# A gated scan with top-k experts on one core: who weighs the scan's input, how the expert weights lie in memory, and where the last scatter may write

## The chip, the cores and the metric

The kernel runs on one core of one Trainium2 chip. The metric is device time in microseconds, the median of several executions. One execution was also recorded by the profiler; all rows below come from it.

## The reference

For each of 4 batches, 6208 tokens of width 256 pass through a gated scan, and then the 128 tokens with the highest score pass through a small two-layer expert. Cut to what matters:

```python
# x, f_logit: [4, 6208, 256] f32; w1: [256, 1024]; w2: [1024, 256]; capacity 128
f = lower_bound + (1.0 - lower_bound) * sigmoid(f_logit)
for t in range(S):
    h = f[:, t] * h + (1.0 - f[:, t]) * x[:, t]
    y[:, t] = h
scores = einsum('bsd,d->bs', y, w_gate)
out = y.copy()
for b in range(B):
    top = argpartition(-scores[b], capacity)[:capacity]
    ye = maximum(y[b, top] @ w1, 0.0) @ w2
    out[b, top] = y[b, top] + sigmoid(scores[b, top])[:, None] * ye
```

## The kernel before

The host lays x and f_logit out with the 256 channels on partitions (two halves of 128) and tokens along the free dimension. A batch is cut into 7 units of 1 to 4 blocks of 256 tokens; the first unit of a batch also takes the 64 tokens left over. There are 28 units and so 56 halves, numbered s = 0 to 55 (unit i has the halves 2i and 2i+1). Halves are 576, 768, 832, 1024 or 256 tokens wide.

For each unit the SyncE queue (SP) loads the forget logits into a tile `ft` (`load_f`, L319; 4 buffers) and x into a tile `xt` (`load_x`, L326; 6 buffers), up to 1 MB each. Then, with r = sigmoid(-f_logit) and ol = 1 - lower_bound:

- `gate` (ScalarE, L335) writes r over `ft` for the whole unit;
- `forget` (ScalarE, L342) writes f = 1 - ol * r into `gt`, a tile in PSUM with two buffers, so it waits for the scan of the half two before;
- the scan's input (1 - f) * x = ol * r * x is made in `xt`. For most halves GpSimd (POOL) does it in two instructions, `prepare` (L345: x * ol) and `weigh` (L353: times r from `ft`). For the seven halves in `SWIFT`, VectorE (DVE) does it in one (L351: x * ol * r, both tensors in SBUF). For the last two halves (`direct`), r is written to PSUM, f back into `ft`, and VectorE reads r from PSUM (L333, L339, L349);
- `scan` (VectorE, L356) runs h = f * h + input along the tokens, f from PSUM, in place in `xt`.

TensorE multiplies the result with the gate vector (`scores`, L369) and transposes it (`turn`, L390). ScalarE copies it to `ym` (`put`, L413; 10 buffers), and SP stores `ym` to the output (`store`, L424; the left-over tokens L427). When a batch's scores are there, VectorE and TensorE search the threshold (`choose`), and `experts` runs: GpSimd gathers the 128 rows from the output in HBM (`fetch`, L736), TensorE transposes them (`flip`, L741) and multiplies with w1 (`up`, L776) and w2 (`down`, L787), VectorE mixes (`mix`, L791), GpSimd scatters the rows back (`scatter`, L795). `flip` of a batch waits for `mix` of the batch before. For the last batch, `fetch` comes behind one tiny memset for each of the last 6 stores (L804), each of which waits until its store has landed.

The weights w1 and w2 (1 MB each) are loaded once (L839, L840), in lines of 4 KB and 1 KB. The last batch finds its rows in a faster way that can be in doubt; then its scatter goes to 128 spare rows behind the end of the output, and a branch does all batches anew. The spare rows are first written by one DMA (`spare_rows`, L836) behind the last store.

The order of every engine's instructions is fixed when the program is built: a planner (`Plan.run`) lists all operations with an engine, an assumed cost, a rank and what they wait for, plays them through, and emits them in the order that comes out. On the chip each engine, and SP's queue too, takes its instructions strictly in that order. Ranks are 10 * s and an offset (`AHEAD` for loads, `STORE` for stores, `TURN` and `PUT` for transposes and their copies, `EXPERT` and `FIND` per batch). `BACKLOG` says how much work the planner lets SP queue ahead. The lines that matter most for SP's order:

```python
add("sp", 0.05 + 2.45 * k, load_f, p - AHEAD, [("weigh", ef), ("scan" if ef < DIRECT[0] else "forget", ef), ("f", i - 1)], ("f", i), late=DONE)
add("sp", 0.05 + 2.45 * k, load_x, p - AHEAD + 1, [("f", i), ("turn", ex - 1), ("turn", ex), ...], ("x", i), late=DONE)
add("sp", ..., store, 20.0 * i + STORE[b] - RUSH.get(i, 0.0), [("put", s), ("put", s - 1), ("store", i - 1)], ("store", i), late=DONE)
```

Here `ef` is the second half of the unit that had the same `ft` buffer, four units before.

Of the kernel before, what the change touches and what calls it, by code (L numbers as in the profile page):

```python
# [17 lines left out]
P = 128  # L18
# [9 lines left out]
DIRECT = (0, 2)  # L28
SWIFT = (9, 13, 17, 21, 25, 29, 53)
XBUF, FBUF, YBUF = 6, 4, 10  # L30
AHEAD = 40.0
BACKLOG, STORE = 3.0, [200.0, 200.0, 200.0, 200.0]
EASED = 1000
LATE, PIECE, SOON, NEAR = 2, 4, 100.0, 5
BIG = ()
TURN, PUT, KEEP, FIND, EXPERT = 0.0, 20.0, 10.0, [0.0, -20.0, -60.0, -100.0], [150.0, 90.0, 100.0, 0.0]
WEIGHTS_AT = 90.0
RUSH = {13: 20.0}
# [22 lines left out]
class Plan:  # L61
# [107 lines left out]
def gated_scan_moe(tc, x, fl, lb, wg, wr, w1, w2, outs, cap):  # L169
    nc = tc.nc  # L170
    v, a, pe, g = nc.vector, nc.scalar, nc.tensor, nc.gpsimd
    with ExitStack() as ctx:
# [128 lines left out]
        def half(s):  # L301
# [8 lines left out]
            direct = s < DIRECT[0] or s >= N - DIRECT[1]  # L310
# [19 lines left out]
            def gate():  # L330
                if direct:
                    gs[s] = pf.tile([P, 4 * BLK], F32, name="gt")
                    a.activation(gs[s][:, :n], fs[s], ACTF.Sigmoid, scale=-1.0)  # L333
                else:
                    a.activation(whole[i], whole[i], ACTF.Sigmoid, scale=-1.0)  # L335

            def forget():
                if direct:
                    a.activation(fs[s], gs[s][:, :n], ACTF.Identity, scale=nl[:, h : h + 1], bias=1.0)  # L339
                    return  # L340
                gs[s] = pf.tile([P, 4 * BLK], F32, name="gt")
                a.activation(gs[s][:, :n], fs[s], ACTF.Identity, scale=nl[:, h : h + 1], bias=1.0)  # L342
# [88 lines left out]
            if h == 0:  # L431
                ef, ex = NH * (i - FBUF) + 1, NH * (i - XBUF) + 1
                oddb = units[i - XBUF] if i >= XBUF else None
                add("sp", 0.05 + 2.45 * k, load_f, p - AHEAD, [("weigh", ef), ("scan" if ef < DIRECT[0] else "forget", ef), ("f", i - 1)], ("f", i), late=DONE)
                add("sp", 0.05 + 2.45 * k, load_x, p - AHEAD + 1, [("f", i), ("turn", ex - 1), ("turn", ex), ("scores", ex), ("odd", oddb[0]) if oddb and oddb[3] else None], ("x", i), late=DONE)
            if direct:
                add("act", 0.15 + 0.85 * k, gate, p, [("f", i), ("scan", s - 2), ("forget", s - 1)], ("gate", s))
                add("dve", 0.15 + 1.07 * k, weigh, p, [("gate", s), ("x", i)], ("weigh", s))
            else:
                if h == 0:  # L440
                    add("act", 0.1 + 0.88 * 2 * k, gate, p, [("f", i)], ("gate", s))
                else:
                    plan.alias(("gate", s), ("gate", s - 1))
                if form == "pool" and s not in SWIFT:
                    add("pool", 0.1 + 1.1 * k, prepare, p, [("x", i)], ("ready", s))
                add("dve" if s in SWIFT else "pool", 0.15 + (1.07 if s in SWIFT else 2.2) * k, weigh, p, [("gate", s), ("ready", s), ("x", i)], ("weigh", s))
            add("act", 0.15 + 0.93 * k, forget, p, [("gate", s), ("scan", s - 2)], ("forget", s))
# [264 lines left out]
        def experts(b, pick=None):  # L712
# [184 lines left out]
        add("sp", 5.0, weights, WEIGHTS_AT, [], ("w",), late=DONE)  # L897
# [26 lines left out]

# [22 lines left out]
```

## Time and profile before

| what | value |
|---|---|
| device time, median of 3 runs | 217.18 us (216.74 to 218.33) |
| the profiled execution's own time | 216.66 us |
| its span, first to last instruction | 214.9 us |
| busy share of the span | PE 78%, DVE 79%, ACT 75%, POOL 77% |
| moved by DMA | 79.84 MB, mean 372 GB/s over the span |
| granted TensorE clock | 0.998 |

The span is the stretch that the rows below count from 0; the profiled execution's own time is 1.8 us longer than the span. A busy share is a mean over the whole span, with a filled stretch and an emptier tail; the GB/s of a stretch say how well the DMA engines were used in it.

### The profile page before, as it was taken

The page shows a single profiled execution, that of the slowest core. Times are in us where ns is not written, and L with a number is a line of the kernel's source. Part 1 is how long each engine was busy: PE and PEld are TensorE (multiplying, and loading weights), DVE is VectorE, ACT ScalarE, POOL GpSimd, SP SyncE. Part 2 cuts the span into 40 slices and gives each one's busy share as a digit, 9 for nine tenths or more (in the row PEclk, how much of TensorE's full clock was granted, in tenths as well). Part 3 has the DMA queues.
Part 4 walks back from the last instruction along what each step waited for, and adds up shares of the span by engine and source line. Part 5 has one row for each costly group of instructions (what it writes and reads, how often), then busy time and mean ns, then how long its engine had stood idle before and what let it go on. Part 6 is the DMA issues. An engine that isn't in the chain of part 4 may idle for free.

```text
span 214.9 us, 3576 instructions
## 1 busy us (share of the span) xinstructions
PE 166.7 (78%) x1188; PEld 106.2 (49%) x1188; DVE 169.2 (79%) x359; ACT 160.3 (75%) x226; POOL 165.2 (77%) x166
## 2 busy tenths in 40 slices
PE   0299986857998879588979967669879878999690
PEld 0043643524455435344548836435547556758570
DVE  2656497979999999999899989688898999891100
ACT  3778899997899899599899778987989378621110
POOL 6699999999795989996999999999999951001201
PEclk9999999999999999999999999999999999999999
DMA  5999999999999999999999999999999999993100
GB/s 179 390 427 421 429 415 392 395 415 419 419 424 418 420 423 418 287 392 412 417 423 422 423 427 421 426 422 421 411 419 411 431 421 424 425 424 117 49 5 31
DMA packets 14568, 79.84 MB, mean 372 GB/s; under 512 B 1873, under 2 KB 3282, under 8 KB 8018
## 3 DMA queue, kind: packets, MB, share of 16 engines
q1 hardware_dynamic: 13872, 78.52, 89.5%
q0 software_dynamic: 384, 1.05, 1.3%
q8 instruction: 11, 0.18, 0.3%
q14 instruction: 11, 0.09, 0.1%
q10 hardware_dynamic: 290, 0.00, 0.1%
HBM read 53.48 MB, written 26.08 MB: 370 GB/s over the span
## 4 chain that ended last, share of the span: by engine, by line
DVE 26%; DMA 25%; POOL 20%; issue 11%; ACT 7%; PE 6%; POOLq 1%; SPq 0%; another core or an unknown queue 0%; DVEq 0%; ACTq 0%
DMA ft<-fl 15%; DVE xt L356 14%; POOL xt L353 12%; POOL xt L345 8%; DMA out<-ym 6%; ACT ft L335 3%; DVE xt L351 3%; DVE ft L627 3%; DMA xt<-x 3%; ACT gt L342 2%; PE pt L390 2%; PE pm L787 2%; ACT ym L413 1%; DMA out<-res,idx 1%; PE pm L776 1%
## 5 line engine op out<-in xcount | busy, mean ns | idle before, releaser
L356 DVE TENSOR_TENSOR_SCAN xt<-gt,xt 128x1024 f32<-128x1024 f32 (+3 forms) x54 | 112.5, 2096 | 17.0 <-POOL xt L353 15.4
L353 POOL TENSOR_TENSOR xt<-xt,ft 128x1024 f32<-128x1024 f32 (+3 forms) x47 | 100.3, 2139 | 4.8 <-POOL xt L345 1.2
L390 PE MATMUL pt<-ident,xt 128*128 128x128 f32 (+1 forms) x392 | 66.7, 305 | 4.6 <-ACT ym L413 3.7
L390 PEld LDWEIGHTS pt<-ident,xt 128*128 128x128 f32 (+1 forms) x392 | 52.7, 202 | 26.2 <-ACT ym L413 15.5
L342 ACT ACTIVATE gt<-ft,nl 128x1024 f32<-128x1024 f32 (+3 forms) x54 | 55.5, 1030 | 9.8 <-DVE xt L356 6.1
L413 ACT COPY ym<-pt 128x512 f32<-128x512 f32 (+1 forms) x104 | 53.7, 556 | 10.0 <-PE pt L390 9.2
L345 POOL TENSOR_SCALAR xt<-xt,ol 128x1024 f32<-128x1024 f32 (+3 forms) x47 | 51.9, 1107 | 8.2 <-DMA xt<-x 6.0
L369 PE MATMUL score<-xt,wgr 128*32 128x256 f32 x380 | 35.7, 403 | 23.9 <-DVE xt L356 20.4
L335 ACT ACTIVATE ft<-ft 128x2048 f32<-128x2048 f32 (+3 forms) x27 | 46.5, 1722 | 5.7 <-DMA ft<-fl 5.5
L906 PE MATMUL score<-wgr 128*32 128x256 f32 x114 | 31.2, 390 | 0.0
L369 PEld LDWEIGHTS score<-xt,wgr 128*32 128x32 f32 x380 | 9.0, 110 | 36.5 <-DVE xt L356 29.5
L776 PE MATMUL pm<-xT,w1t 128*128 128x128 f32 x128 | 16.2, 281 | 0.0
L776 PEld LDWEIGHTS pm<-xT,w1t 128*128 128x128 f32 x128 | 14.9, 192 | 1.7 <-ACT xT L745 0.8
L787 PE MATMUL pm<-w2t,hT 128*128 128x256 f32 x64 | 14.9, 383 | 0.0
L906 PEld LDWEIGHTS score<-wgr 128*32 128x32 f32 x114 | 10.1, 109 | 9.4 <-issue 1.6
L787 PEld LDWEIGHTS pm<-w2t,hT 128*128 128x128 f32 x64 | 11.7, 191 | 1.5
L351 DVE SCALAR_TENSOR_TENSOR xt<-xt,ol,ft 128x1024 f32<-128x1024 f32 (+2 forms) x7 | 12.1, 1723 | 0.0
L791 DVE SCALAR_TENSOR_TENSOR res<-pm,open,xe 128x256 f32<-128x256 f32 x4 | 1.9, 481 | 12.3 <-PE pm L787 12.3
L804 POOL MEMSET ym<- 1x1 f32 x6 | 0.6, 94 | 13.6 <-DMA out<-ym 11.1
L736 POOL DMA_INDIRECT xe<-out,idx x4 | 4.4, 1100 | 7.9 <-DMA out<-ym 6.6
L782 ACT ACTIVATE hT<-pm 128x512 f32<-128x512 f32 x8 | 4.8, 594 | 5.1 <-PE pm L776 5.1
L795 POOL DMA_INDIRECT out<-res,into x1 | 1.0, 979 | 9.4 <-DVE res L791 9.4
(153 smaller groups left out, 109.7 us busy)
## 6 DMA issues: line engine op xcount, KB each, us to landing
ft<-fl SPq DMA_DIRECT2D x17, 1024.0 KB, 11.2
xt<-x SPq DMA_DIRECT2D x17, 1024.0 KB, 12.8
out<-ym SPq DMA_DIRECT2D x17, 1024.0 KB, 13.3
out<-ym SPq DMA_DIRECT2D x7, 768.0 KB, 15.4
ft<-fl SPq DMA_DIRECT2D x6, 768.0 KB, 8.2
xt<-x SPq DMA_DIRECT2D x6, 768.0 KB, 9.6
ft<-fl SPq DMA_DIRECT2D x3, 576.0 KB, 10.5
xt<-x SPq DMA_DIRECT2D x3, 576.0 KB, 8.6
```

What stands on the lines that cost most here:

```text
L335: a.activation(whole[i], whole[i], ACTF.Sigmoid, scale=-1.0)
L342: a.activation(gs[s][:, :n], fs[s], ACTF.Identity, scale=nl[:, h : h + 1], bias=1.0)
L345: g.tensor_scalar(xs[s], xs[s], ol[:, h : h + 1], 1.0, ALU.mult, ALU.mult)
L351: v.scalar_tensor_tensor(xs[s], xs[s], 1.0 if form == "pe" else ol[:, h : h + 1], fs[s], ALU.mult, ALU.mult)
L353: g.tensor_tensor(xs[s], xs[s], fs[s], ALU.mult)
L356: v.tensor_tensor_scan(xs[s], fs[s] if direct else gs[s][:, :n], xs[s], carry[h] if blk0 else 0.0, ALU.mult, ALU.add)
L369: pe.matmul(score[j * CG : (j + 1) * CG, b % 2], row(b, h, r), xs[s][:, c : c + BLK], start=(h == 0 and r == 0), stop=(h == NH - 1 and blk ...
L390: pe.transpose(out, src, ident)
L413: copy(yms[i][:, j0:j1, rows], pts[s, j0][:, : (j1 - j0) * P].rearrange("p (j d) -> p j d", d=P))
L776: pe.matmul(st["pm", f // TP][:, c : c + P], w1t[:, h, f * P : (f + 1) * P], st["xT"][:, h], start=(h == 0), stop=(h == NH - 1))
L787: pe.matmul(st["py"][:, :D], st["hT"][:, f], w2t[:, f], start=(f == 0), stop=(f == NF - 1))
L906: pe.matmul(score[:CG, 0], wgr[:, 0, CG : 2 * CG], wgr.rearrange("p a c -> p (a c)"), start=False, stop=True, skip_group_check=True)
```

## The change

Fourteen halves in place of nine are weighed by VectorE, now from f in PSUM: it computes (f - 1) * x, which is minus the scan's input, and the scan subtracts it. So such a half doesn't read `ft` after `forget`, and its weigh waits for `forget`. The special form of the last two halves goes. The weights are folded by the host so that each partition reads one line of 8 KB. The last scatter is given the end of the output as a bound and skips indices beyond it, so the spare rows and the DMA that writes them go. Some of the planner's assumed costs and constants change, so the order on every queue is planned anew.

```diff
-DIRECT = (0, 2)
-SWIFT = (9, 13, 17, 21, 25, 29, 53)
+SWIFT = (0, 1, 2, 3, 9, 13, 17, 21, 25, 29, 33, 53, 54, 55)
-BACKLOG, STORE = 3.0, [200.0, 200.0, 200.0, 200.0]
+BACKLOG, STORE = 4.0, [200.0, 200.0, 200.0, 200.0]
-LATE, PIECE, SOON, NEAR = 2, 4, 100.0, 5
+LATE, PIECE, SOON, NEAR = 4, 2, 100.0, 5
-TURN, PUT, KEEP, FIND, EXPERT = 0.0, 20.0, 10.0, [0.0, -20.0, -60.0, -100.0], [150.0, 90.0, 100.0, 0.0]
+TURN, PUT, KEEP, FIND, EXPERT = 10.0, 30.0, 10.0, [0.0, -20.0, -60.0, -100.0], [60.0, 120.0, 200.0, 0.0]
...
             def weigh():
-                if direct:
-                    v.scalar_tensor_tensor(xs[s], xs[s], 1.0 if form == "pe" else ol[:, h : h + 1], gs[s][:, :n], ALU.mult, ALU.mult)
-                elif s in SWIFT:
-                    v.scalar_tensor_tensor(xs[s], xs[s], 1.0 if form == "pe" else ol[:, h : h + 1], fs[s], ALU.mult, ALU.mult)
+                if swift:
+                    v.scalar_tensor_tensor(xs[s], gs[s][:, :n], 1.0, xs[s], ALU.subtract, ALU.mult)
                 else:
                     g.tensor_tensor(xs[s], xs[s], fs[s], ALU.mult)
 
             def scan():
-                v.tensor_tensor_scan(xs[s], fs[s] if direct else gs[s][:, :n], xs[s], carry[h] if blk0 else 0.0, ALU.mult, ALU.add)
+                v.tensor_tensor_scan(xs[s], gs[s][:, :n], xs[s], carry[h] if blk0 else 0.0, ALU.mult, ALU.subtract if swift else ALU.add)
...
-                add("sp", 0.05 + 2.45 * k, load_f, p - AHEAD, [("weigh", ef), ("scan" if ef < DIRECT[0] else "forget", ef), ("f", i - 1)], ("f", i), late=DONE)
+                add("sp", 0.05 + 2.45 * k, load_f, p - AHEAD, [*(("weigh", q) for q in (ef - 1, ef) if q not in SWIFT), ("forget", ef), ("f", i - 1)], ("f", i), late=DONE)
...
+            if swift:
+                add("dve", 0.15 + 1.07 * k, weigh, p - HASTE, [("forget", s), ("x", i)], ("weigh", s))
+            else:
+                add("pool", 0.1 + 1.03 * k, prepare, p, [("x", i)], ("ready", s))
+                add("pool", 0.15 + 2.22 * k, weigh, p, [("gate", s), ("ready", s), ("x", i)], ("weigh", s))
+            add("act", 0.15 + 0.97 * k, forget, p, [("gate", s), ("scan", s - 2)], ("forget", s))
...
-                g.indirect_dma_start(out=outs[b][:, :], out_offset=to, in_=st["res"][:cap, :], in_offset=None)
+                g.indirect_dma_start(out=outs[b][:, :], out_offset=to, in_=st["res"][:cap, :], in_offset=None,
+                                     **(dict(bounds_check=S - 1, oob_is_err=False) if planned and b == B - 1 else {}))
...
-        def spare_rows():
-            nc.sync.dma_start(outs[B - 1][S:, :], wgr.rearrange("p a c -> p (a c)"))
-
         def weights():
-            nc.sync.dma_start(w1t, w1.rearrange("(h p) f -> p h f", p=P))
-            nc.sync.dma_start(w2t, w2.rearrange("(k p) d -> p k d", p=P))
+            nc.sync.dma_start(w1t.rearrange("p h f -> p (h f)"), w1)
+            nc.sync.dma_start(w2t.rearrange("p k d -> p (k d)"), w2)
...
-        add("sp", 0.3, spare_rows, 1e6, [("store", len(units) - 1)], ("spare",), late=DONE)
...
+def folded(w):
+
+    return np.ascontiguousarray(w.reshape(-1, P, w.shape[1]).transpose(1, 0, 2).reshape(P, -1))
```

The halves 0 to 3 and 33 move from GpSimd to VectorE; 9, 13, 17, 21, 25, 29 and 53 stay on VectorE in the new form; 54 and 55 were the two `direct` ones.

## Rows read from the trace of the kernel before

**Rows 1.** The page's second part: GB/s in 40 equal slices of 5.37 us.
```profile
GB/s 179 390 427 421 429 415 392 395 415 419 419 424 418 420 423 418 287 392 412 417 423 422 423 427 421 426 422 421 411 419 411 431 421 424 425 424 117 49 5 31
```

**Rows 2.** Busy time by stretch; the last three columns: clock, DMA share, GB/s.
```profile
36.00:40.00 4.00, 2.65 (x27) 1.64 (x28) 4.00 (x3) 4.00 (x7) 3.92 (x3) 1.00 1.08 367
40.00:84.00 44.00, 35.58 (x272) 20.67 (x271) 42.10 (x82) 40.31 (x56) 39.46 (x27) 1.00 1.02 420
84.00:92.00 8.00, 5.75 (x43) 3.08 (x42) 7.86 (x11) 5.70 (x8) 7.75 (x8) 1.00 0.93 307
92.00:192.00 100.00, 83.40 (x630) 55.75 (x629) 89.94 (x207) 79.40 (x117) 79.60 (x56) 1.00 1.01 421
```

**Rows 3.** Timeline of SP's queue, w2's load and around 80 us: start, us, instruction.
```profile
24.13 0.46 SPq L840 DMA_DIRECT2D w2t<-w  x1
...
75.58 0.33 SPq L319 DMA_DIRECT2D ft<-fl  x1
...
76.55 0.77 SPq L424 DMA_DIRECT2D out<-ym  x1
...
85.68 0.33 SPq L319 DMA_DIRECT2D ft<-fl  x1
```

**Rows 4.** SP's own waits from 60 to 96 us: total, times, longest.
```profile
SPq L319 <- DVE xt L351: 15.9, 3, 8.2
```

**Rows 5.** Timeline of GpSimd, ScalarE and VectorE beside two of VectorE's weighs.
```profile
28.64 2.33 DVE L351 SCALAR_TENSOR_TENSOR xt<-xt,ol,ft 128x1024 f32<-128x1024 f32 x1
...
29.87 2.09 POOL L345 TENSOR_SCALAR xt<-xt,ol 128x1024 f32<-128x1024 f32 x1
...
79.75 4.70 POOL L353 TENSOR_TENSOR xt<-xt,ft 128x1024 f32<-128x1024 f32 x2 [0.80 <-POOL xt L345]
...
82.56 1.12 ACT L342 ACTIVATE gt<-ft,nl 128x1024 f32<-128x1024 f32 x1
...
83.21 2.32 DVE L351 SCALAR_TENSOR_TENSOR xt<-xt,ol,ft 128x1024 f32<-128x1024 f32 x1
```

**Rows 6.** Groups by line and shape: count, busy us, mean ns, idle before.
```profile
L356 DVE TENSOR_TENSOR_SCAN xt<-gt,xt 128x1024 f32<-128x1024 f32 x34 | 79.1, 2342 | 8.0 <-POOL xt L353 7.9
...
L353 POOL TENSOR_TENSOR xt<-xt,ft 128x768 f32<-128x768 f32 x11 | 21.0, 1912 | 1.1 <-ACT ft L335 0.4
...
L345 POOL TENSOR_SCALAR xt<-xt,ol 128x768 f32<-128x768 f32 x11 | 9.9, 905 | 0.3 <-DMA xt<-x 0.3
L351 DVE SCALAR_TENSOR_TENSOR xt<-xt,ol,ft 128x1024 f32<-128x1024 f32 x5 | 9.7, 1938 | 0.0
...
L627 DVE SCALAR_TENSOR_TENSOR ft<-gt,most 128x768 f16<-128x768 f32 x7 | 6.7, 956 | 0.4 <-PE gt L624 0.2
...
L349 DVE SCALAR_TENSOR_TENSOR xt<-xt,ol,gt 128x256 f32<-128x256 f32 x2 | 0.9, 470 | 0.2 <-ACT ft L339 0.2
```

**Rows 7.** DMA issues by line, the load of w2: KB, us from issue to landing.
```profile
w2t<-w SPq DMA_DIRECT2D x1, 1024.0 KB, 17.1
```

**Rows 8.** Timeline of the tail; in brackets the idle time before and its releaser.
```profile
188.39 0.61 SPq L424 DMA_DIRECT2D out<-ym  x1
...
189.05 1.07 SPq L836 DMA_DIRECT2D out<-wgr  x1
...
192.76 0.16 DVE L640 SCALAR_TENSOR_TENSOR idx<-pulled 128x1 int32<-128x1 f32 x1
...
197.04 0.09 POOL L804 MEMSET ym<- 1x1 f32 x1 [0.57 <-DMA out<-ym]
...
198.12 0.97 POOL L736 DMA_INDIRECT xe<-out,idx  x1 [0.99 <-DMA out<-wgr]
...
198.87 0.48 DVE L791 SCALAR_TENSOR_TENSOR res<-pm,open,xe 128x256 f32<-128x256 f32 x1 [4.30 <-PE pm L787]
...
200.96 0.41 PE L741 MATMUL pm<-ident,xe 128*128 128x128 f32 x2 [1.65 <-DMA xe<-out,idx]
...
210.00 0.98 POOL L795 DMA_INDIRECT out<-res,into  x1 [9.36 <-DVE res L791]
```

More of the change, by code (lines that the diff above doesn't have):

```diff
@@ L27 @@
 FORMS = [["pool", "pool"]] * 4
-DIRECT = (0, 2)
-SWIFT = (9, 13, 17, 21, 25, 29, 53)
+SWIFT = (0, 1, 2, 3, 9, 13, 17, 21, 25, 29, 33, 53, 54, 55)
 XBUF, FBUF, YBUF = 6, 4, 10
 AHEAD = 40.0
-BACKLOG, STORE = 3.0, [200.0, 200.0, 200.0, 200.0]
+BACKLOG, STORE = 4.0, [200.0, 200.0, 200.0, 200.0]
 EASED = 1000
-LATE, PIECE, SOON, NEAR = 2, 4, 100.0, 5
+LATE, PIECE, SOON, NEAR = 4, 2, 100.0, 5
 BIG = ()
-TURN, PUT, KEEP, FIND, EXPERT = 0.0, 20.0, 10.0, [0.0, -20.0, -60.0, -100.0], [150.0, 90.0, 100.0, 0.0]
+TURN, PUT, KEEP, FIND, EXPERT = 10.0, 30.0, 10.0, [0.0, -20.0, -60.0, -100.0], [60.0, 120.0, 200.0, 0.0]
 WEIGHTS_AT = 90.0
+HASTE = 0.0
 RUSH = {13: 20.0}
@@ L309, in half @@
             k = n / 1024
-            direct = s < DIRECT[0] or s >= N - DIRECT[1]
+            swift = s in SWIFT
             form = FORMS[b][h]
@@ L330, in gate @@
             def gate():
-                if direct:
[L332 to L335, printed above, removed]
+                a.activation(whole[i], whole[i], ACTF.Sigmoid, scale=-1.0)
             def forget():
-                if direct:
-                    a.activation(fs[s], gs[s][:, :n], ACTF.Identity, scale=nl[:, h : h + 1], bias=1.0)
-                    return
                 gs[s] = pf.tile([P, 4 * BLK], F32, name="gt")
@@ L347, in weigh @@
             def weigh():
-                if direct:
-                    v.scalar_tensor_tensor(xs[s], xs[s], 1.0 if form == "pe" else ol[:, h : h + 1], gs[s][:, :n], ALU.mult, ALU.mult)
-                elif s in SWIFT:
-                    v.scalar_tensor_tensor(xs[s], xs[s], 1.0 if form == "pe" else ol[:, h : h + 1], fs[s], ALU.mult, ALU.mult)
+                if swift:
+                    v.scalar_tensor_tensor(xs[s], gs[s][:, :n], 1.0, xs[s], ALU.subtract, ALU.mult)
                 else:
@@ L433, in half @@
                 oddb = units[i - XBUF] if i >= XBUF else None
-                add("sp", 0.05 + 2.45 * k, load_f, p - AHEAD, [("weigh", ef), ("scan" if ef < DIRECT[0] else "forget", ef), ("f", i - 1)], ("f", i), late=DONE)
+                add("sp", 0.05 + 2.45 * k, load_f, p - AHEAD, [*(("weigh", q) for q in (ef - 1, ef) if q not in SWIFT), ("forget", ef), ("f", i - 1)], ("f", i), late=DONE)
                 add("sp", 0.05 + 2.45 * k, load_x, p - AHEAD + 1, [("f", i), ("turn", ex - 1), ("turn", ex), ("scores", ex), ("odd", oddb[0]) if oddb and oddb[3] else None], ("x", i), late=DONE)
-            if direct:
-                add("act", 0.15 + 0.85 * k, gate, p, [("f", i), ("scan", s - 2), ("forget", s - 1)], ("gate", s))
-                add("dve", 0.15 + 1.07 * k, weigh, p, [("gate", s), ("x", i)], ("weigh", s))
-            else:
[L440 to L447, printed above, removed]
+                add("act", 0.1 + 0.9 * 2 * k, gate, p, [("f", i)], ("gate", s))
+            else:
+                plan.alias(("gate", s), ("gate", s - 1))
+            if swift:
[4 more added lines that the diff above has]
+            add("act", 0.15 + 0.97 * k, forget, p, [("gate", s), ("scan", s - 2)], ("forget", s))
             add("dve", 0.1 + 2.24 * k, scan, p, [("forget", s), ("weigh", s), ("scan", s - 2)], ("scan", s))
@@ L896, in gated_scan_moe @@
             half(s)
-        add("sp", 5.0, weights, WEIGHTS_AT, [], ("w",), late=DONE)
+        add("sp", 4.9, weights, WEIGHTS_AT, [], ("w",), late=DONE)
         add("pe", 0.4, spread_row, -1e3, [("x", 0)], ("row",), frees=("kept row",))
         add("act", 0.37, keep_row, -1e3, [("row",)], ("kept row",))
-        add("sp", 0.3, spare_rows, 1e6, [("store", len(units) - 1)], ("spare",), late=DONE)
         for b in range(B):
@@ L936 @@
         "wr": np.ascontiguousarray(moe_w_gate.reshape(1, D)),
-        "w1": np.ascontiguousarray(moe_w1),
-        "w2": np.ascontiguousarray(moe_w2),
+        "w1": folded(moe_w1),
+        "w2": folded(moe_w2),
     }
@@ L941 @@
     args = [nc.dram_tensor(n, arr.shape, F32, kind="ExternalInput").ap() for n, arr in arrays.items()]
-    outs = [nc.dram_tensor(f"out{b}", (S + P * (b == B - 1), D), F32, kind="ExternalOutput").ap() for b in range(B)]
+    outs = [nc.dram_tensor(f"out{b}", (S, D), F32, kind="ExternalOutput").ap() for b in range(B)]
     with tile.TileContext(nc, schedule_with_timeline_sim=True) as tc:
```

## Prediction

> **What bounds the kernel now.** I read the page's slices first, because a busy share over the whole span hides stages. The transfer rate is near 420 GB/s from the second slice to 193 us, except for one slice of 287 and its neighbour of 392, with shallower dips to 395 and 392 around 32 to 43 us [rows 1]. The table by stretch sharpens that: 420 over 40 to 84 us, 421 over 92 to 192 us, at a DMA share of 1.0, but 307 over 84 to 92 us and 367 over 36 to 40 us [rows 2]. No compute engine is that full. So the DMA stream sets the time to about 197 us, and what counts is bytes, slow bytes and holes in it.
>
> SP's queue shows where the hole comes from. After a load at 75.58 us and a store at 76.55 us it issues nothing until 85.68 us [rows 3]; its own waits name VectorE's weigh L351, with 8.2 us as the longest [rows 4]. That weigh reads `ft`, so the next load into the buffer waits for it, and the stores behind the load in SP's fixed order wait too. When SP goes on, the engines have run low.
>
> The tail comes third. The last store is issued at 188.39 us and the spare rows at 189.05 us; the last of the tiny memsets, which waits for the last store, runs at 197.04 us, and the last gather only at 198.12 us, after 0.99 us of waiting for the spare rows' DMA [rows 8]. Gather, expert and scatter then run in series to the end, hidden by nothing.
>
> **The change, part by part.**
>
> *Spare rows gone.* The gather needs the last store but no longer the DMA that overlapped it in name only: 0.99 us off the tail [rows 8]. What is late next is the expert of batch 2: its mix ends at 198.87 + 0.48 = 199.35 us, and the last expert's transposes, which wait for it, ran at 200.96 us [rows 8]. So up to 1.6 us may be gained in front of this mix without touching it; what goes beyond needs the mix to move as well. It should: its gather waits for a store, which moves with the stream.
>
> *Weights in 8 KB lines.* w2, in 1 KB lines, was issued at 24.13 us [rows 3] and landed 17.1 us later, at 41.2 us [rows 7], so it moved at the end of that stretch. At 36 to 40 us the rate was 367 with a DMA share of 1.08: the engines were full but slow. Against the 421 of the long stretch that is (421 - 367) / 421 x 4 = 0.5 us [rows 2]. I take 0.5, with 0 and, for the edges of the dip, 0.8 as ends. The Trainium skill speaks against it: "DMA: Bandwidth & Descriptors", section Specifications, puts line rate at transfers of 512 B and more, so 1 KB lines would cost nothing, folding would gain nothing, and the sum below would be 0.5 us smaller. The row says otherwise.
>
> *The hole.* Its price is (421 - 307) / 421 x 8 = 2.2 us [rows 2]. The load that ended it waited for the weigh that ran 83.21 to 85.53 us. In the new form it would wait for `forget`, done at 82.56 + 1.12 = 83.68 us, and for GpSimd's weigh of the half before, done at 79.75 + 4.70 = 84.45 us [rows 5]. That alone is 1.1 us earlier with nothing else moved. The engines ahead of it move too. VectorE was busy 42.1 of 44 us over 40 to 84 us [rows 2], so what it saves there lets buffers go earlier. A weigh of 1024 took 1.94 us on average [rows 6] and up to 2.33, and one beside it on GpSimd, L345, took 2.09 us [rows 5], against some 905 x 1024 / 768 = 1.2 us by its narrower form [rows 6]: they held each other up.
>
> *The new weigh.* No row shows this form at 1024. The two nearest, with one operand in PSUM, are L349 (256 wide, 0.47 us) and L627 (768 wide, 0.956 us) [rows 6]; their slope, 0.95 ns per element, gives 1.20 us at 1024 and 0.77 at 576 (estimates). Both ran while GpSimd did next to nothing, so the other end is the contended 2.33 us [rows 5]. I take 1.20: the scan, too, has one operand in PSUM and one in SBUF, and holds a mean of 2.34 us over 34 instances beside GpSimd [rows 6]. [...]
>
> For the seven halves that stay (five of 1024, one 768, one 576) that is 5 x 1.20 + 0.96 + 0.77 = 7.7 us in place of some 12.1 (the five of 1024 took 9.7 [rows 6]). The five that come to VectorE (0 to 3, 33: two of 576, three of 768) cost 2 x 0.77 + 3 x 0.96 = 4.4 us. So VectorE's total stays as it is, with relief in the first search and new work at the start, where GpSimd held it up. GpSimd loses three halves at 0.905 + 1.912 = 2.8 us [rows 6] and two of 576 at three quarters of that, 12.7 us in all, and the mutual hold-ups. Beside the DMA stream all this is worth nothing by itself; it counts only through the hole.
>
> *New wait.* A weigh on VectorE now waits for `forget`, which waits for the scan two halves before. Queued behind it on VectorE are the next scans and search steps, and TensorE and SP's buffers wait for those. `forget` took 1.12 us [rows 5] and the scan between takes 2.34 [rows 6], so it is ready in time unless ScalarE is late. I cost it at nothing; without that cover it is up to 1.1 us for each of the 14, and matters only where VectorE is already full.
>
> *The scan that subtracts, the gate of the last unit, the bound on the scatter.* The same pass with another operation: 0. The last unit's gate and weigh sit some 10 us ahead of the last store's landing, behind queued stores: 0. The scatter at 210.00 us takes 0.98 us to issue [rows 8]; the bound may cost between nothing and as much again, 1.0, and a little below nothing can't be excluded. I take 0, since nothing suggests a second pass over the indices.
>
> *The new order.* It is not in the trace. The planner's assumed costs and constants change for every queue, so the hole may vanish, shrink or reappear elsewhere. Of 2.2 us I take 1.7, nearer to the full price than to the 1.1 us of the dependence alone.
>
> **Sum.** 1.0 (spare rows) + 0.5 (weights) + 1.7 (hole) = 3.2 us off 216.66 us for an execution like the profiled one. That one lies 0.5 us under the median of the runs, so the median goes from 217.18 to 214.0 us.
>
> **Rivals.**
>
> *The hole stays.* SP blocks again for longer than what it has queued. For it: SP's order is fixed, and stores stand behind loads. Against it: the awaited weigh is shorter and no longer what `ft` waits for. Only 1.5 us remain: 215.7.
>
> *The gain is given back by batch 2's expert.* `EXPERT` ranks it behind the last transposes now (200 in place of 100). If its mix stays at 199.35 us, the last transposes can move from 200.96 to about 199.55 at best, so only 1.4 us is kept: 215.8. Against it: the transposes had ended before its rows arrived.
>
> *Slower.* SP's queue blocks behind a load in a later search as well, where VectorE has 89.9 of 100 us of work [rows 2] and half 33 adds 0.96. Each such hole costs 2.2 us. With the old one kept, two new ones give 217.18 - 1.5 + 4.4 = 220.1; it decides once the new waits hold SP longer than the some 8 us between the store at 76.55 us and the fall of the rate at 84. Against it: the whole stretch from 92 us runs at 421 without one hole.
>
> *All goes well.* Hole 2.2, weights 0.8, spare rows 1.0: 4.0 us, 213.2 or, if the order also fills the edges, a little below.
>
> *It doesn't do what it says:* the weigh beside GpSimd still takes 2.33. Then VectorE has 5 x 1.13 us and more on top of the estimates; in the first search that keeps the hole, the first rival's time.
>
> **How the numbers follow.** Forecast, 213.5 to 215: 0.50. All well or better: 0.12. Hole stays (also through a slow weigh): 0.18. Given back: 0.11. Slower: 0.09. The range goes from 212.0, which adds 1 us to the best case for what a new order can do, to 217.5, no gain with the spread of the runs. Measurement tells about 1% (2.2 us) from no change: below 215.0 is faster, above 219.4 slower. The forecast and the best case lie below 215.0, the two middle rivals between. That gives faster 0.62, same 0.29, slower 0.09.
>
> **What the new profile would show.** The slice at 86 us near 420 and no wait of SP on a weigh of VectorE over 2 us; no dip around the weights' arrival; weighs of about 1.20 us at 1024 beside a busy GpSimd, and no L345 at 2.1 us; the last gather within 0.2 us of the last tiny memset, some 3 us earlier; the mix of batch 2 ahead of the last transposes. The prediction is wrong if the stream has a hole elsewhere, if search or the mix, not the last store, releases the last gather or transposes (the last indices came at 192.76 us [rows 8], 4 us before the last memset), or if the last scatter takes 2 us to issue.

## The result, and the profile after

The kernel before took 217.37 us (median of 20 runs, 216.28 to 219.16), the changed one 215.22 us (20 runs, 213.78 to 217.28): a ratio of 0.988, with an interval of 0.9855 to 0.9908, so about 2.6 us or 1.2% faster. The ratio is that of the means, 217.61 and 215.03 us, without the one slow execution of the changed kernel (217.28 us); the medians are 2.15 us apart. The profiled execution of the changed kernel took 214.37 us, with a span of 212.5 us and a granted clock of 0.996; the one before had a span of 214.9 us.

The page's second part, GB/s in 40 equal slices of 5.31 us, is the counterpart of [rows 1]:

```profile
GB/s 175 394 425 424 422 418 422 412 416 417 422 415 424 414 425 428 424 419 422 421 424 417 422 423 427 419 422 433 420 416 414 431 416 429 421 395 45 49 5 31
```

Neither the slice of 287 nor the dip to 392 and 395 is left: from the third slice to the 35th the rate stays between 412 and 433. The table by stretch of the changed kernel, which answers to [rows 2] (busy time of TensorE, its weight loads, VectorE, ScalarE and GpSimd with the number of instructions, then clock, DMA share, GB/s):

```profile
36.00:40.00 4.00, 2.69 (x27) 1.35 (x25) 4.00 (x3) 4.00 (x6) 3.92 (x3) 1.00 1.00 414
40.00:84.00 44.00, 36.40 (x267) 20.88 (x267) 39.83 (x88) 38.75 (x53) 36.30 (x27) 1.00 1.02 420
84.00:92.00 8.00, 5.83 (x42) 2.98 (x41) 7.45 (x4) 6.91 (x9) 6.49 (x7) 1.00 1.01 424
92.00:188.00 96.00, 80.12 (x610) 53.70 (x611) 85.77 (x199) 77.82 (x115) 73.62 (x52) 1.00 1.01 423
```

367 became 414, 307 became 424, and the long stretches stayed as they were. The hole was not all idle DMA engines. In the kernel before, its two halves read:

```profile
84.00:88.00 4.00, 3.09 (x16) 1.43 (x14) 3.86 (x9) 3.11 (x4) 3.92 (x5) 1.00 0.85 332
88.00:92.00 4.00, 2.66 (x27) 1.65 (x28) 4.00 (x3) 2.60 (x4) 3.83 (x4) 1.00 1.01 283
```

The engines were idle for part of the first half only (share 0.85); in the second, after SP had gone on, they were busy (share 1.01) and moved 283 GB/s. Both halves run at 424 in the changed kernel. Why the transfers are slow behind the pause no run shows; the price of the hole counts both.

SP's queue, by its timeline around 80 us and, in the second fence, by its own waits from 60 to 96 us (total, times, longest), says how; these answer to [rows 3, 4]:

```profile
75.70 0.33 SPq L319 DMA_DIRECT2D ft<-fl  x1
...
76.87 0.71 SPq L415 DMA_DIRECT2D out<-ym  x1
81.13 0.33 SPq L319 DMA_DIRECT2D ft<-fl  x1
```

```profile
SPq L319 <- ACT gt L335: 29.2, 6, 6.1
SPq L319 <- POOL xt L344: 0.5, 2, 0.2
```

The load that was issued at 85.68 us [rows 3] is issued at 81.13 us. SP still waits in front of it, for 3.5 us, but for ScalarE's `forget` (L335 here) and no longer for VectorE's weigh; the 6.1 us are the longest of six such waits, in front of another load. The stretch of this queue without an issue is 3.55 us long (76.87 + 0.71 to 81.13), not 8.4 us (76.55 + 0.77 to 85.68 before), and what was queued covers it: 424 GB/s over 84 to 92 us.

The timeline of the three engines around that load shows what the new form gained. The load goes into the buffer of halves 24 and 25; `forget` of half 25 is L335 at 79.94 us, its weigh on VectorE L342:

```profile
79.94 1.13 ACT L335 ACTIVATE gt<-ft,nl 128x1024 f32<-128x1024 f32 x1
80.18 2.34 DVE L347 TENSOR_TENSOR_SCAN xt<-gt,xt 128x1024 f32<-128x1024 f32 x1
80.27 2.35 POOL L344 TENSOR_TENSOR xt<-xt,ft 128x1024 f32<-128x1024 f32 x1
...
83.41 1.21 DVE L342 SCALAR_TENSOR_TENSOR xt<-gt,xt 128x1024 f32<-128x1024 f32 x1
```

`ft` is free when `forget` ends, at 81.07 us, and SP issues 0.06 us later. The weigh ends at 84.62 us: a read of `ft` by it would have held the load for another 3.55 us. In the kernel before, `forget` of half 25 is the second line here:

```profile
80.12 2.34 DVE L356 TENSOR_TENSOR_SCAN xt<-gt,xt 128x1024 f32<-128x1024 f32 x1
...
80.47 1.13 ACT L342 ACTIVATE gt<-ft,nl 128x1024 f32<-128x1024 f32 x1
```

The scan is that of half 24, the last one in front of half 25's weigh. The `forget` at 82.56 us [rows 5] starts 0.1 us after this scan has ended; `forget` waits for the scan two halves before, so it is half 26's, and half 25's is the one at 80.47 us. It ended at 81.60 us, 3.93 us before the weigh did (85.53 us). In the changed kernel it ends 0.53 us earlier.

Groups by line and shape (count, busy us, mean ns, idle before), to be read beside [rows 6]:

```profile
L347 DVE TENSOR_TENSOR_SCAN xt<-gt,xt 128x1024 f32<-128x1024 f32 x34 | 79.3, 2343 | 9.5 <-POOL xt L344 8.8 <-issue 0.4
...
L338 POOL TENSOR_SCALAR xt<-xt,ol 128x1024 f32<-128x1024 f32 x29 | 32.4, 1120 | 3.4 <-ACT ym L404 2.2 <-DMA xt<-x 1.1
...
L342 DVE SCALAR_TENSOR_TENSOR xt<-gt,xt 128x1024 f32<-128x1024 f32 x5 | 6.0, 1209 | 0.0
...
L342 DVE SCALAR_TENSOR_TENSOR xt<-gt,xt 128x768 f32<-128x768 f32 x4 | 3.8, 939 | 0.0
L342 DVE SCALAR_TENSOR_TENSOR xt<-gt,xt 128x576 f32<-128x576 f32 x3 | 2.2, 748 | 0.5 <-ACT gt L335 0.5
```

The new weigh takes 1.209 us at 1024 beside a busy GpSimd, waits for `forget` for 0.5 us in all, and the 34 scans of 1024, five of which now subtract, take 2.343 us on average, as the 34 that add did (2.342); the one behind the weigh at 83.41 us took 2.35. GpSimd's own multiplication holds 1.120 us at 1024.

The tail, by the timeline of GpSimd, VectorE and TensorE (in brackets the idle time before and its releaser), answers to [rows 8]:

```profile
194.74 0.09 POOL L793 MEMSET ym<- 1x1 f32 x1 [0.55 <-DMA out<-ym]
195.59 0.96 POOL L724 DMA_INDIRECT xe<-out,idx  x1 [0.76 <-issue]
195.77 0.48 DVE L779 SCALAR_TENSOR_TENSOR res<-pm,open,xe 128x256 f32<-128x256 f32 x1 [2.96 <-PE pm L775]
...
198.46 0.41 PE L729 MATMUL pm<-ident,xe 128*128 128x128 f32 x2 [2.24 <-DMA xe<-out,idx]
...
207.50 1.01 POOL L783 DMA_INDIRECT out<-res,into  x1 [9.64 <-DVE res L779]
```

The last memset comes at 194.74 us in place of 197.04 (2.30 us earlier: the stream) and the last gather at 195.59 in place of 198.12 (2.53 us earlier, so 0.23 us for the spare rows). From gather to scatter it is 11.91 us, 11.88 before; from the scatter to the end of the span 5.0 us, 4.9 before. The whole gain is there before the last gather.

### The profile page after: what moved, and what is told of

It reads as the page before. It is cut to its first block, busy times and chain, and to the rows that moved or that the text cites. A ratio compares the mean times of both kernels' runs of the same rounds, so it can differ in the third digit from the quotient of the medians.

```text
span 212.5 us, 3559 instructions
## 1 busy us (share of the span) xinstructions
PE 165.6 (78%) x1188; PEld 105.6 (50%) x1188; DVE 168.2 (79%) x364; ACT 160.1 (75%) x225; POOL 147.6 (69%) x156
## 4 chain that ended last, share of the span: by engine, by line
DMA 33%; POOL 22%; ACT 14%; DVE 11%; issue 11%; PE 6%; POOLq 1%; ACTq 0%; SPq 0%; another core or an unknown queue 0%
POOL xt L344 12%; DMA ft<-fl 12%; DMA xt<-x 12%; DVE xt L347 8%; POOL xt L338 8%; ACT ft L331 6%; DMA out<-ym 4%; ACT gt L335 4%; ACT ym L404 4%; PE pt L381 3%; DMA wgt<-wg 3%; DVE xt L342 2%; POOL xe L724 2%; PE score L360 1%; DMA out<-res,idx 1%
## 5 line engine op out<-in xcount | busy, mean ns | idle before, releaser
L347 DVE TENSOR_TENSOR_SCAN xt<-gt,xt 128x1024 f32<-128x1024 f32 (+4 forms) x56 | 114.4, 2050 | 16.0 <-POOL xt L344 12.0
L344 POOL TENSOR_TENSOR xt<-xt,ft 128x1024 f32<-128x1024 f32 (+3 forms) x42 | 91.1, 2174 | 3.7 <-issue 1.3
L381 PE MATMUL pt<-ident,xt 128*128 128x128 f32 (+1 forms) x392 | 66.0, 304 | 6.4 <-ACT ym L404 3.6
L381 PEld LDWEIGHTS pt<-ident,xt 128*128 128x128 f32 (+1 forms) x392 | 52.6, 202 | 26.2 <-ACT ym L404 14.9
L335 ACT ACTIVATE gt<-ft,nl 128x1024 f32<-128x1024 f32 (+4 forms) x56 | 56.5, 1012 | 7.5 <-DVE xt L347 4.8
L338 POOL TENSOR_SCALAR xt<-xt,ol 128x1024 f32<-128x1024 f32 (+3 forms) x42 | 43.8, 1045 | 20.6 <-DMA xt<-x 15.2
L331 ACT ACTIVATE ft<-ft 128x2048 f32<-128x2048 f32 (+4 forms) x28 | 47.2, 1686 | 9.0 <-DMA ft<-fl 8.0
L360 PE MATMUL score<-xt,wgr 128*32 128x256 f32 x380 | 36.3, 404 | 22.1 <-DVE xt L347 15.3
L764 PE MATMUL pm<-xT,w1t 128*128 128x128 f32 x128 | 16.2, 281 | 0.0
L764 PEld LDWEIGHTS pm<-xT,w1t 128*128 128x128 f32 x128 | 14.9, 192 | 1.7 <-ACT xT L733 1.2
L775 PE MATMUL pm<-w2t,hT 128*128 128x256 f32 x64 | 15.0, 382 | 0.3 <-ACT hT L770 0.3
L342 DVE SCALAR_TENSOR_TENSOR xt<-gt,xt 128x1024 f32<-128x1024 f32 (+3 forms) x14 | 12.8, 917 | 0.5 <-ACT gt L335 0.5
L775 PEld LDWEIGHTS pm<-w2t,hT 128*128 128x128 f32 x64 | 11.7, 190 | 2.1 <-ACT hT L770 0.8
```

The lines of the kernel that those rows point to most:

```text
L338: g.tensor_scalar(xs[s], xs[s], ol[:, h : h + 1], 1.0, ALU.mult, ALU.mult)
L342: v.scalar_tensor_tensor(xs[s], gs[s][:, :n], 1.0, xs[s], ALU.subtract, ALU.mult)
L347: v.tensor_tensor_scan(xs[s], gs[s][:, :n], xs[s], carry[h] if blk0 else 0.0, ALU.mult, ALU.subtract if swift else ALU.add)
L360: pe.matmul(score[j * CG : (j + 1) * CG, b % 2], row(b, h, r), xs[s][:, c : c + BLK], start=(h == 0 and r == 0), stop=(h == NH - 1 and blk ...
L381: pe.transpose(out, src, ident)
L764: pe.matmul(st["pm", f // TP][:, c : c + P], w1t[:, h, f * P : (f + 1) * P], st["xT"][:, h], start=(h == 0), stop=(h == NH - 1))
```

## The experiments

The theory after these readings: the form of the weigh fills the hole, because `ft` is free after `forget`, before VectorE comes to the weigh. Rivals: the new order does it and the form doesn't matter; or the form does, but by ending the hold-ups between VectorE and GpSimd. Open beside these: what lines, spare rows, constants and the five added halves are worth. A time and a ratio are against the kernel before on the same chip; the last memset marks the end of the stream. All line numbers are those of the kernel run.

**The changed kernel again, for comparison.**

> The changed kernel once more, as the yardstick for the runs beside it. All theories: about 2.5 us under the kernel before, last tiny memset near 194.7 us, last gather near 195.6 us.

Measured: 215.18 us, ratio 0.9886 (0.9854 to 0.9917); last memset 194.60 us, last gather 195.44 us. This execution's last scatter came at 208.95 us all the same, 1.45 us later than in the profile above. The table by stretch shows why, in the clock (third column from the end):

```profile
196.00:200.00 4.00, 1.75 (x11) 1.17 (x11) 0.51 (x3) 0.47 (x2) 1.40 (x2) 0.96 0.20 66
200.00:204.00 4.00, 4.00 (x24) 4.00 (x24) 0.00 (x0) 0.60 (x1) 0.00 (x0) 0.61 0.00 0
```

TensorE was busy for 1.75 of 4 us while the last gather was under way, and then its granted clock was 0.61, so part of that stretch ran at the lower of its two levels, 1.2 GHz. The 32 matmuls of the last `up` took 5.47 us there and 3.84 us in the profile above. The same program has both tails.

**Weights in the old lines.**

```diff
-nc.sync.dma_start(w1t.rearrange("p h f -> p (h f)"), w1)
+nc.sync.dma_start(w1t, w1.rearrange("(h p) f -> p h f", p=P))
```

(and the same for w2, with the host's folding gone.)

> The changed kernel with the weights read in lines of 4 KB and 1 KB again, same order on every queue. Theory (1 KB lines are slow): a dip to some 365 to 375 GB/s around the landing of the second weight, near 36 to 42 us, and the last tiny memset 0.4 to 0.6 us later than in the changed kernel, 195.1 to 195.3 us. Rival (lines of 512 B and more are at full rate): no dip, memset at 194.7 within 0.2 us.

Measured: 216.29 us, 0.9938 (0.9906 to 0.9969). The dip is back, at the same place and to the same depth as in [rows 2]:

```profile
36.00:40.00 4.00, 2.69 (x27) 1.42 (x26) 4.00 (x3) 4.00 (x5) 3.92 (x3) 1.00 1.08 366
```

The last memset is at 195.15 us, 0.55 us later than in the comparison run. That is what the lines are worth to the stream, by one profile of each (the two profiles of the changed kernel differ by 0.14 us there); the medians differ by 1.1 us, and the rest is not shown. The Trainium skill ("DMA: Bandwidth & Descriptors", section Specifications) puts line rate at 512 B and more. Here the stretch in which w2 moved ran at 366 GB/s with its lines of 1 KB and at 414 to 416 with lines of 8 KB, so the measurement decides against it.

**The spare rows and the unbounded scatter.**

```diff
-                g.indirect_dma_start(out=outs[b][:, :], out_offset=to, in_=st["res"][:cap, :], in_offset=None,
-                                     **(dict(bounds_check=S - 1, oob_is_err=False) if planned and b == B - 1 else {}))
+                g.indirect_dma_start(out=outs[b][:, :], out_offset=to, in_=st["res"][:cap, :], in_offset=None)
...
+            nc.sync.dma_start(outs[B - 1][S:, :], wgr.rearrange("p a c -> p (a c)"))
```

> The changed kernel with the spare rows written again behind the last store, and the last scatter without a bound; same order otherwise. Theory (the gather's 0.99 us of idle time before was mostly its own lead, which the changed kernel still shows as 0.76 us): the last gather starts 0.2 to 0.3 us later after the last tiny memset, gap 1.0 in place of 0.76, span longer by 0.2 to 0.3 us. Rival (the prediction's term): the gather waits a whole 1.0 us more, gap 1.7. The bound on the scatter: issue time of the last scatter 0.98 in place of 1.015 us.

Measured: 216.44 us, 0.9931 (0.9897 to 0.9964). The last gather, in the timeline of GpSimd:

```profile
194.58 0.09 POOL L792 MEMSET ym<- 1x1 f32 x1 [0.57 <-DMA out<-ym]
195.66 0.96 POOL L724 DMA_INDIRECT xe<-out,idx  x1 [0.99 <-PE pm L775]
...
209.16 0.97 POOL L783 DMA_INDIRECT out<-res,into  x1 [11.23 <-DVE res L779]
```

The idle time in front of the gather is 0.99 us, as in [rows 8], where the changed kernel has 0.76: 0.23 us for the spare rows. It is 0.94 to 1.00 us in all four profiles with spare rows and 0.72 to 0.76 in all ten without. The scatter without a bound takes 0.97 us to issue, with one 1.01: the bound costs 0.04 us. That this scatter comes as late as 209.16 us is the clock again: 0.58 over 200 to 204 us in this profile. The median is 1.3 us above that of the comparison run; 0.2 of it is shown, the rest is not, and the intervals of the two ratios overlap.

**The old form in the new order.** Same set of 14 halves, same order on every queue.

```diff
-v.scalar_tensor_tensor(xs[s], gs[s][:, :n], 1.0, xs[s], ALU.subtract, ALU.mult)
+v.scalar_tensor_tensor(xs[s], xs[s], ol[:, h : h + 1], fs[s], ALU.mult, ALU.mult)
...
-v.tensor_tensor_scan(xs[s], gs[s][:, :n], xs[s], carry[h] if blk0 else 0.0, ALU.mult, ALU.subtract if swift else ALU.add)
+v.tensor_tensor_scan(xs[s], gs[s][:, :n], xs[s], carry[h] if blk0 else 0.0, ALU.mult, ALU.add)
```

> The changed kernel with the fourteen halves weighed from r in SBUF as before (x times ol times r, scan adds), same order on every queue. Theory (the form matters: two SBUF operands make VectorE and GpSimd hold each other up, and the load into ft waits for VectorE's weigh): weighs of 1024 take 1.7 to 2.3 us in place of 1.21, GpSimd's L338 up to 2.1 beside them, SP waits for L342, and a hole of 1 to 2 us opens again in the first search, so 1 to 2 us slower than the changed kernel. Rival (only the new order removed the hole): weighs are slower but the rate at 84 to 92 us stays near 420 and the time stays within 0.4 us of the changed kernel.

Measured: 217.90 us, 1.0022 (1.0001 to 1.0043). The whole gain is gone, and the hole is back, with the wait that belongs to it (the table by stretch, then SP's own waits from 60 to 96 us):

```profile
40.00:84.00 44.00, 37.35 (x283) 21.20 (x275) 41.67 (x85) 40.37 (x55) 37.26 (x26) 1.00 1.01 409
84.00:92.00 8.00, 6.01 (x52) 3.51 (x44) 7.83 (x8) 5.79 (x7) 7.75 (x8) 1.00 0.89 310
```

```profile
SPq L319 <- DVE xt L342: 15.0, 2, 7.6
```

The last memset is at 197.76 us, 3.2 us later than in the comparison run. The hole is 2.1 us of that, by the prediction's formula; some 1.1 us more go where 40 to 84 us ran at 409 GB/s in place of 420. So the new order by itself does nothing against the hole, and with the old form it loses time in a second place; the form does it.

**The new form, but SP waits for VectorE.** Behind each new weigh VectorE copies one column of `ft`, so that the buffer is again free only when VectorE has passed the weigh. All else, the order too, is that of the changed kernel.

```diff
 v.scalar_tensor_tensor(xs[s], gs[s][:, :n], 1.0, xs[s], ALU.subtract, ALU.mult)
+v.tensor_copy(seen, fs[s][:, :1])
```

> The changed kernel, same order, with one copy of a single column of ft on VectorE behind each of the fourteen weighs (0.1 us each; its result is not used). The weigh keeps its new form, so nothing holds GpSimd up, but the load into ft waits for VectorE again. It splits what the old form cost. Theory A (SP's wait for VectorE opens the hole): rate at 84 to 92 us under 350, memset 196.5 us or later. Theory B (the mutual hold-up of VectorE and GpSimd makes the engines late): the copies cost little, rate above 410, memset within 0.4 us of 194.7.

Measured: 216.59 us, 0.9962 (0.9919 to 1.0004). The table by stretch, then the timeline around the load, then the group of the weigh:

```profile
84.00:92.00 8.00, 6.57 (x52) 3.70 (x46) 7.93 (x9) 5.93 (x7) 6.81 (x7) 1.00 0.95 315
```

```profile
81.05 1.13 ACT L336 ACTIVATE gt<-ft,nl 128x1024 f32<-128x1024 f32 x1
...
84.42 1.22 DVE L343 SCALAR_TENSOR_TENSOR xt<-gt,xt 128x1024 f32<-128x1024 f32 x1
...
85.55 0.14 DVE L344 COPY seen<-ft 128x1 f32<-128x1 f32 x1
...
85.84 0.33 SPq L320 DMA_DIRECT2D ft<-fl  x1
```

```profile
L339 POOL TENSOR_SCALAR xt<-xt,ol 128x1024 f32<-128x1024 f32 x29 | 32.4, 1121 | 3.1 <-ACT ym L406 2.3 <-PE score L893 0.8
```

The load goes out behind the copy, 4.7 us later than in the changed kernel and 3.5 us after `forget` of that half has ended (82.18 us), and the rate over 84 to 92 us is 315. The 14 copies are 2.0 us of VectorE in all. The weigh keeps its short form and GpSimd's multiplication its 1.12 us, so there is no hold-up here, and the hole is there all the same; the last memset is at 197.38 us, 2.8 us later than in the comparison run. This settles the two readings of the form: it is the read of `ft`, not the hold-up. The hold-up adds at most what the run before has beyond this one, 0.4 us at the last memset.

**The old kernel with its store ahead of the blocking load.** The sixth store is ranked 40 earlier.

```diff
-RUSH = {13: 20.0}
+RUSH = {5: 40.0, 13: 20.0}
```

> The kernel before with one change: SP issues the sixth store ahead of the load that blocked it, so that 1 MB (2.5 us of transfer) is queued when it blocks. Weighs stay in the old form. Theory (the hole is SP's queue blocked behind a load while stores are ready): the hole at 84 to 92 us shrinks from 2.2 us to under 1 us and the last tiny memset comes 1.2 to 2.2 us earlier than 197.0. Rival (VectorE and GpSimd are simply behind and the hole only moves): the same 2 us are missing in another stretch, memset at 197.0 within 0.4 us.

Measured: 216.71 us, 0.9933 (0.9896 to 0.9970). SP waits for VectorE as before (L351, 7.5 us the longest) and issues the load at 86.00 us, but with one store more in the queue:

```profile
84.00:92.00 8.00, 5.76 (x45) 3.08 (x42) 7.86 (x11) 5.70 (x8) 7.75 (x8) 1.00 1.01 413
92.00:188.00 96.00, 83.29 (x628) 55.32 (x624) 82.80 (x191) 79.78 (x117) 79.06 (x55) 1.00 1.01 418
```

With the queue filled, 84 to 92 us runs at a share of 1.01 and 413 GB/s. A part of the hole moved to a later stretch (418, in place of 421); the last memset is at 195.70 us, 1.34 us earlier than in [rows 8]. So the hole can also be narrowed from its other side, and that it costs time is shown without touching the form.

**The old constants, and the old set, each in the changed kernel.** In the first, `BACKLOG`, `LATE`, `PIECE`, `TURN`, `PUT`, `EXPERT` and the planner's costs are those of before; in the second the five added halves go back to GpSimd.

```diff
-SWIFT = (0, 1, 2, 3, 9, 13, 17, 21, 25, 29, 33, 53, 54, 55)
+SWIFT = (9, 13, 17, 21, 25, 29, 53, 54, 55)
```

> The changed kernel with the planner's constants and assumed costs of before (backlog 3, late 2, pieces of 4, ranks of transposes, copies and experts, and the costs of gate, forget, prepare and weigh). SP's order differs from the changed kernel's in one store. Theory (the form of the weigh removed the hole, the constants did little): rate at 84 to 92 us above 410, last tiny memset within 0.4 us of 194.7, time within 0.5 us of the changed kernel. Rival (the new constants did it): the hole is back, 1.5 to 2 us slower.

> The changed kernel with halves 0 to 3 and 33 weighed by GpSimd as before; nine halves on VectorE in the new form, order planned anew. Theory (those five are beside the stream): time within 0.5 us of the changed kernel, GpSimd busy some 12 us more. Rival (GpSimd's 12.7 us of relief feed the stream): rates under 410 in some stretch before 92 us and 1 us or more slower.

Measured: 214.21 us, 0.9830 (0.9784 to 0.9877) with the old constants, and 214.84 us, 0.9880 (0.9829 to 0.9931) with the old set. The rate over 84 to 92 us is 424 and 426, the last memset at 194.52 and 194.28 us. Neither the constants nor the five halves contribute to the gain. The old constants look 1 us better than the new, by the ratios too (0.983 against 0.988), but the intervals of the two kernels overlap.

**Both together**, once with the new form alone in the old kernel (old lines, spare rows), and once with the lines and the bound kept.

> The kernel before with the new form of the weigh alone, on its seven halves and the last two: weights in 4 KB and 1 KB lines, spare rows, old constants and costs; the planner knows that the load no longer waits for these weighs. Theory (the form makes the gain): no hole at 84 to 92 us (above 410 GB/s), the dip at 36 to 40 us still there near 367, last tiny memset 195.0 to 195.4 us, time 1.5 to 2.2 us under the kernel before. Rival (the form needs the rest of the change): hole still there, within 0.5 us of the kernel before.

> The new form on the nine halves, weights in 8 KB lines and no spare rows, with the old constants, costs and set of halves. Theory: everything that gains is in it, so the last tiny memset near 194.5 us and the time within 0.4 us of the changed kernel or under it. Rival (set or constants carry part of it together): 0.7 us or more slower than the changed kernel.

Measured: 222.33 us, 1.0186 (1.0132 to 1.0241), and 221.61 us, 1.0158 (1.0104 to 1.0213): slower by 4 to 5 us, which none of the theories had. The hole is filled in both (424 and 422 over 84 to 92 us). The loss is in the tail. In the timeline of the second kernel, TensorE, ScalarE and GpSimd:

```profile
191.82 3.70 PE L775 MATMUL pm<-w2t,hT 128*128 128x256 f32 x16
...
195.35 0.39 PE L381 MATMUL pt<-ident,xt 128*128 128x128 f32 x2
195.78 0.37 ACT L404 COPY ym<-pt 128x256 f32<-128x256 f32 x1 [3.47 <-PE pt L381]
...
196.70 0.37 ACT L404 COPY ym<-pt 128x256 f32<-128x256 f32 x1 [0.55 <-PE pt L381]
199.63 0.09 POOL L793 MEMSET ym<- 1x1 f32 x1 [2.26 <-DMA out<-ym]
```

In the order that the planner made of this combination, batch 2's expert (L764 and L775, from 186.74 us) stands ahead of the last transposes of the last unit (L381 at 195.35 us). Their copies end at 197.07 us, the last store leaves only then, and the last memset runs at 199.63 us: 4.9 us later than in the changed kernel, with the DMA engines at 14 GB/s over 192 to 196 us. In the run with the old constants and the new set the last transposes stand between `flip` and `up` of that expert, and the last copy starts at 187.66 us:

```profile
186.99 0.64 PE L381 MATMUL pt<-ident,xt 128*128 128x128 f32 x2
187.65 3.16 PE L764 MATMUL pm<-xT,w1t 128*128 128x128 f32 x16
```

The late gather then finds TensorE idle for most of 196 to 204 us, its granted clock is 0.50 over 204 to 208 us, and the last `up` takes 5.55 us, 1.7 us more than in the profile of the changed kernel. 4.9 + 1.7 = 6.6 us is nearly all of what the span is longer (219.3 against 212.5 us).

**Fillers for TensorE in front of the last expert**, six matmuls in the changed kernel, and five in the one with the old constants.

```diff
 def flip():
     st["px"] = psum()
+    if planned and b == B - 1:
+        for _ in range(6):
+            spin()
```

> The changed kernel with six more filler matmuls on TensorE while it waits for the last gather (nothing else reads their result). In one profile of the changed kernel the granted clock was 0.61 at 200 to 204 us, after a stretch with 1.75 us of work in 4, and the last expert took 1.6 us longer than in the other. Theory (the idle stretch lets the clock fall in part of the executions): from last gather to last scatter 11.9 us as in the better profile, and the median falls by 0.4 to 0.8 us under the changed kernel. Rival (the fall has nothing to do with that idle stretch, or the fillers delay the transposes): no gain, or 0.3 us slower.

> The changed kernel with the old constants and costs (214.2 us in one series) and five filler matmuls in front of the last expert's transposes, as a candidate that is faster than both. Theory: no execution with a fall of the clock in the last expert, median 213.7 to 214.2 us. Rival: the fillers gain nothing or delay by 0.3 us, 214.2 to 214.6 us.

Measured: 214.96 us, 0.9859 (0.9812 to 0.9906), and 214.22 us, 0.9818 (0.9766 to 0.9869). In both profiled executions the clock over 200 to 204 us was 1.00; from gather to scatter it was 12.24 and 12.05 us, up to 0.3 us more than the 11.91 of the changed kernel. With six fillers TensorE has no idle time left in front of the transposes, so the rows wait for the fillers; with five it still waits 0.36 us for the rows. Against the same kernels without fillers (ratios 0.9886 and 0.9830) there is no gain that these runs can tell. The lowest medians of all are those of the old constants, 214.21 us without and 214.22 us with fillers, some 1 us below the changed kernel, with intervals that overlap its own.

## Why the prediction was right, and where its terms were off

It said 214.0 us with a range of 212.0 to 217.5, and the median was 215.2: inside the range, but 0.2 us above the band of 213.5 to 215 to which it gave a chance of 0.50, and above 215.0, its own line for faster. The gain was 2.6 us by the ratio, 2.15 by the medians and 2.4 by the profiled spans, where its sum was 3.2. The stream's part of that sum, 0.5 + 1.7 = 2.2 us, lies within 0.1 us of the 2.30 measured, in part by luck: the hole was put 0.5 us too low, for a reason that was misread, and hole and weights together brought some 0.4 us less than their two prices. Term by term:

- **What bounds the kernel: right.** The last memset moved by 2.30 us, and all that follows it, from gather to end, moved by the same within 0.3 us.
- **The hole, 1.7 us of 2.2: the mechanism right, the size 0.5 us too low, for a misread reason.** It came in full: (424 - 307) / 421 x 8 = 2.2 us. That the load waits for VectorE's weigh, and in the new form for `forget` alone, is what the runs show. But the step took the wrong instructions for what the load would wait for: the `forget` that ended at 83.68 us is half 26's, and GpSimd's weighs that ended at 84.45 us are those of halves 26 and 27 (that of half 24 had to end before its scan began at 80.12 us). The `forget` that counts ended at 81.60 us, so the dependence alone was worth 3.9 us and not 1.1. The load came 4.55 us forward, 0.5 us of it by an earlier `forget`. Read rightly, the step would have spoken for the full price. It also gave half of its reason to the hold-ups between VectorE and GpSimd; the run that keeps the read and has no hold-up shows the hole whole.
- **The weights, 0.5 us: right.** (414 - 367) / 421 x 4 = 0.45 us by the table by stretch, 0.55 us by the run with the old lines. Together with the hole that would be 2.65 to 2.75 us, and 2.30 came: the two overlap, or a little is lost later; no run tells which.
- **The spare rows, 1.0 us: the term that was mis-sized.** They gave 0.23 us. The step read the 0.99 us of idle time in front of the gather [rows 8] as waiting for the DMA that the row names. 0.76 us of it is still there when that DMA is gone, with "issue" as its releaser: the indirect DMA starts that much behind the memset with nothing to wait for. The term is 0.77 us too large, nearly the whole distance from 3.2 to 2.4 us, what the profiled span lost. The last gather is 0.85 us behind the last memset, not within the 0.2 us that the prediction looked for.
- **The new weigh, 1.20 us at 1024 and 0.77 at 576: right** (1.209 and 0.748), beside a busy GpSimd. All 14 take 12.8 us. The Trainium skill ("SBUF — State Buffer", section "SBUF: two separate sides") describes a lock for which a VectorE instruction with two SBUF inputs and a GpSimd instruction that reads SBUF contend. These rows agree with it: with one of VectorE's operands in PSUM, GpSimd's multiplication holds 1.12 us, where it took up to 2.09 before [rows 5].
- **The wait for `forget`, 0: right** (0.5 us of idle time in all, off the path). **The scan that subtracts, 0: right** (2.34 to 2.35 us at 1024, where those that add had a mean of 2.342 [rows 6]). **The bound, 0: right** (0.04 us).
- **The rivals.** The hole didn't stay, and batch 2's expert gave nothing back: its mix ended at 196.25 us, 2.2 us ahead of the last transposes, which waited for their rows. The slower rival, a second hole by the new order, did not come either. But an order that loses 5 us exists close by: the old constants with the old set. There the loss is not a blocked load, as the rival had it, but batch 2's expert ahead of the last transposes on TensorE. The prediction put no price on that.

What stays open: why the medians with the old lines and with the spare rows are 1.1 and 1.3 us above the changed kernel, when stream and gather account for 0.55 and 0.2 us of it. With the 2.7 us of the old form that makes 5.1 us, twice the whole gain, so these differences are not shares of it. The mean granted clock of these executions is lower (medians 0.976 and 0.973, against 0.986 in the comparison run), but where in an execution it fell is known only for the one that was profiled, and a low clock in the stream need not cost: with the old constants it was 0.88 over 40 to 84 us at 419 GB/s. From the last scatter's start to the span's end it is 4.6 to 5.7 us over the fourteen profiles, 5.6 and 5.5 in these two runs and 4.9 in the comparison run; one profile of each doesn't tell whether the change or chance does that. Which of the old constants, with the old set, puts the expert ahead was not tried either.

## What to carry to other kernels

A hole in the DMA stream is closed by finding what the queue's next load waits for and asking which engine reads that buffer last: here a weigh that reads its factor from PSUM frees the buffer an engine earlier, which was worth 2.2 us, though VectorE's own time hardly changed (169.2 us busy before, 168.2 after). Idle time in front of an instruction is not all waiting for the releaser that its row names: compare it with the same instruction where nothing holds it, before it goes into a sum. Where the order is planned, a new form has to be planned and looked at with its constants: the new form with folded weights and the bound gave 1.2% in one order and took 1.6% in another, by which work stood ahead of the last transposes.

## What the runs showed of the hardware

- The TensorE clock in the tail is not the same in all executions of one program. With TensorE busy for 1.76 of 4 us over 196 to 200 us the granted clock stayed at 1.00 in the first profile of the changed kernel; with 1.75 of 4 it fell to 0.61 in the second, and 32 matmuls took 1.6 us more. It fell over the same 4 us in two more of the fourteen profiles (0.58 with the spare rows, 0.61 with the store ahead). Where TensorE had been busy for 0.5 of 4 us over 196 to 200 us (both slower kernels) it was 0.50 over 204 to 208 us.
- The last gather, an indirect DMA on GpSimd, starts 0.72 to 0.76 us behind the memset before it in all ten profiles in which it has nothing to wait for; the scatter of batch 2 behind this gather has 0.30 us in the changed kernel.
- Behind a pause in the queue the DMA engines can be busy and slow: share 1.01 at 283 GB/s over 88 to 92 us in the kernel before, 424 GB/s at the same share in the changed one.
- While w2 moves in lines of 1 KB the DMA engines are full (share 1.08) at 366 to 368 GB/s, in all four profiles with such lines; with 8 KB lines the same stretch gives 409 to 416 at a share of 0.99 to 1.01.
